# Reordering the first group of a fused FFT and GEGLU backward kernel: dO transposes, w_down products, and the life of q

## The chip, the cores and the metric

The kernel runs on one core of one Trainium2 chip. The metric is the device time of one execution in microseconds. The engines of the core are TensorE (PE, matrix products and transposes; PEld is its weight load), VectorE (DVE), ScalarE (ACT), GpSimd (POOL) and SyncE (SP, which issues transfers). They run side by side and wait for each other by semaphores.

## The reference, cut to what matters

The forward pass mixes two branches with a gate computed from `x`: a filter in the frequency domain (`a`) and a GEGLU feed-forward (`b`). Both branches and the gate read the same `x`; the input `B_x` is not used. The kernel computes the output and the gradients of the seven inputs that are used.

```python
# x: 2048 x 576, w_gate, w_up: 576 x 4608, w_down: 4608 x 576, all bf16
g = sigmoid((x * gate_w).sum(-1))
X = rfft2(x) * (w_r + 1j * w_i)
a = irfft2(X)
b = (gelu(x @ w_gate) * (x @ w_up)) @ w_down
out = g * a + (1 - g) * b
# gradients of out . grad_out for x, w_r, w_i, w_gate, w_up, w_down, gate_w
```

For the feed-forward branch the backward pass needs, with dO the incoming gradient: `z = dO @ w_down^T` (scaled by 1 - g it is `da`), the products A = gelu(xg) * xu, dH_g and dH_u, and then the weight gradients `d_w_down = A^T @ ((1-g) dO)` and `d_w_gate`, `d_w_up` = `x^T @ [dH_g, dH_u]`.

## The kernel before

The first part of the kernel goes over 18 groups of 256 hidden columns. Each group is four steps (m = 0 to 3), and a step takes 512 of the 2048 rows. So "step 9" is the first step of the third group, and the steps are counted from `pr = 0` in the code. One step makes z (16 matmuls over 128 rows of d each and 4 over the last 64), xy (gate and up products, in two halves, each in a PSUM tile of two), evacuates these with ScalarE, and works out the GELU and its derivative on VectorE. The weight gradients of a group are made in the four steps of the next group, as a list of jobs; a list of Fourier units (`fft_next`) is spread between the jobs. The z tile and the Fourier units' tile are one and the same PSUM buffer.

```python
pz = tc.tile_pool(name="pz", bufs=1, space=PSUM)    # z and the Fourier units' tile
pg = tc.tile_pool(name="pg", bufs=2, space=PSUM)    # first group: transposes and gate
pw = tc.tile_pool(name="pw", bufs=2, space=PSUM)    # later groups: weight gradients ("wps")
# ... cut ...
def H_mm(g, m, between=()):
    for t in ts:                                    # 4 x 4 matmuls of z
        for ci in range(4):
            nc.tensor.matmul(zo(t), lhsT=dOT[:, ci, t, :], rhs=wdT[:, ci, :], ...)
    for f in between:
        f()
    for t in ts:                                    # z: the last 64 rows of d; L418
        nc.tensor.matmul(zo(t), lhsT=dOT[r, 4, t, :], rhs=wdT[r, 4, :], ...)
    # ... xy: the last 64 rows of d (L422); full(k) makes the rest of half k (L429)
```

The chain on VectorE has a first part (`H_ew1`: s, q, the start of dH_g) and a second (`H_ew2`) behind the sigmoids. The tile q exists once from the second group on; ScalarE writes it from xy (`Square`, L448) in `H_act`.

```python
def H_ew2(g, m, tiles, s, dH, da):
    xb, q, hu = tiles
    one = g < 2 or m == 2
    if one:
        om = xb
        nc.scalar.activation(s[:], s[:], ACT.Sigmoid, scale=2.0 * C_GELU)
    else:
        om, s = s, ewt("sg", g)
        nc.scalar.activation(s[:], om[:], ACT.Sigmoid, scale=2.0 * C_GELU)
        nc.scalar.activation(om[:], om[:], ACT.Sigmoid, scale=-2.0 * C_GELU)
    A = keepA.tile([P, 4, FG], BF16, tag="A", name="A")
    dHg, dHu = dH[:, :, 0, :], dH[:, :, 1, :]
    V.tensor_tensor(xb[:], xb[:], s[:], op=ALU.mult)          # L483
    V.tensor_tensor(dHu, da[:], xb[:], op=ALU.mult)           # L484
    V.tensor_tensor(A[:], xb[:], hu[:], op=ALU.mult)          # L485
    V.tensor_tensor(q[:], xb[:], q[:], op=ALU.mult)           # L486
    if one:
        V.tensor_scalar(om[:], s[:], -1.0, 1.0, op0=ALU.mult, op1=ALU.add)
    V.tensor_tensor(om[:], om[:], q[:], op=ALU.mult)          # L489, last reader of q
    V.tensor_tensor(om[:], om[:], s[:], op=ALU.add)
    V.tensor_tensor(dHg, dHg, om[:], op=ALU.mult)
```

The jobs of a group are dealt to its steps by this list (entries 0 to 3: steps of the next group; entry 4: carried into the first step of the group after; entry 5: placed inside a step, before xy). `d` are the four products of d_w_down (two halves of 8 matmuls each, L535), `w` the four of d_w_gate and d_w_up (in quarters of 4 matmuls, L553).

```python
if g == 0:
    return [[w[0][:1], w[1][:1]], [w[2]], [d[0], d[1], d[2], d[3]], [w[3][:3]], w[3][3:],
            {1: [w[0][1][1], w[1][1][1]], 2: [tail]}]
```

And these are the first group's and the later groups' steps:

```python
if g == 0:
    z, xy_full = H_mm(g, m, ([opening] if m == 0 else []) + rest)
    rest = []
    da = H_da(g, m, z)
    # do2, x1: three transposing items each; dO of step m + 2, x of step m + 1
    if m == 0:
        early, mid_, late_ = do1[:2], [do1[2], x1[0]], x1[1:]
    elif m < NPR - 1:
        early, mid_, late_ = x1[:2], x1[2:], []
    for f in early: f()
    xy = xy_full(0)
    for f in mid_: f()
    # ... H_act of half 0, second half of xy, H_act of half 1 ...
    if m < NPR - 1:
        gate(m + 1)
    if m + 2 < NPR:
        do2[0]()
        do2[1]()
        rest = [do2[2]]
    state += [*H_ew1(g, tiles, da), da]
else:
    z, xy_full = H_mm(g, m)
    da = H_da(g, m, z)
    # ... inside ...
    xy = xy_full(0)
    if held:
        scale_dB(0, AC)      # (1-g) dO, rows of one quarter, on ScalarE (AC) or VectorE (VC)
        held.pop()()
    # ... H_act of half 0, xy_full(1), H_act of half 1 ...
    state += [*H_ew1(g, tiles, da), da]
    if pr == 5:
        scale_dB(1, AC)
        scale_dB(2, VC)
        build_R(nc, tb, unit, 8)
        build_R(nc, tb, unit, 12)
    elif pr == 6:
        scale_dB(3, VC)
        next(makeB)
    # ... the jobs of the step, with Fourier units between them; then H_ew2 ...
```

After the 18 groups a second part reads A and dH back from memory and makes the output and the gradient of x.

Of the kernel before, what the change touches and what calls it, by code (L numbers as in the profile page):

```python
# [10 lines left out]
ALU = mybir.AluOpType  # L11
# [244 lines left out]
def kernel(  # L256
# [7 lines left out]
    V = nc.vector  # L264
# [168 lines left out]
    def ewt(tag, g):  # L433
        if tag in ("q", "s", "sg"):
            return unit([4, FG], name=tag) if g == 0 else ew.tile([P, 4, FG], BF16, tag=tag, name=tag, bufs=1)
        return ew.tile([P, 4, FG], BF16, tag=tag, name=tag, bufs=2)
# [7 lines left out]
    def H_act(k, xy, tiles, part):  # L444
        xb, q, hu = tiles
        h = slice(2 * k, 2 * k + 2)
        if part == 0:
            nc.scalar.activation(q[:, h, :], xy[:, :, 0:FG], ACT.Square)  # L448
        else:
            nc.scalar.copy(xb[:, h, :], xy[:, :, 0:FG])  # L450
            nc.scalar.copy(hu[:, h, :], xy[:, :, FG:2 * FG])  # L451

    def H_ew1(g, tiles, da):
        xb, q, hu = tiles
        s = ewt("s", g)
        V.tensor_scalar(s[:], q[:], A_GELU, 1.0, op0=ALU.mult, op1=ALU.add)  # L456
        V.tensor_tensor(s[:], xb[:], s[:], op=ALU.mult)
        V.tensor_scalar(q[:], q[:], 6.0 * A_GELU * C_GELU, 2.0 * C_GELU, op0=ALU.mult, op1=ALU.add)
        dH = keep.tile([P, 4, 2, FG], BF16, tag="dH", name="dH")
        V.tensor_tensor(dH[:, :, 0, :], da[:], hu[:], op=ALU.mult)  # L460
        return s, dH
# [9 lines left out]
    def H_ew2(g, m, tiles, s, dH, da):  # L471
        xb, q, hu = tiles
        one = g < 2 or m == 2
        if one:
            om = xb
            nc.scalar.activation(s[:], s[:], ACT.Sigmoid, scale=2.0 * C_GELU)
        else:
            om, s = s, ewt("sg", g)
            nc.scalar.activation(s[:], om[:], ACT.Sigmoid, scale=2.0 * C_GELU)  # L479
            nc.scalar.activation(om[:], om[:], ACT.Sigmoid, scale=-2.0 * C_GELU)  # L480
        A = keepA.tile([P, 4, FG], BF16, tag="A", name="A")
        dHg, dHu = dH[:, :, 0, :], dH[:, :, 1, :]
        V.tensor_tensor(xb[:], xb[:], s[:], op=ALU.mult)  # L483
        V.tensor_tensor(dHu, da[:], xb[:], op=ALU.mult)  # L484
        V.tensor_tensor(A[:], xb[:], hu[:], op=ALU.mult)  # L485
        V.tensor_tensor(q[:], xb[:], q[:], op=ALU.mult)  # L486
        if one:
            V.tensor_scalar(om[:], s[:], -1.0, 1.0, op0=ALU.mult, op1=ALU.add)
        V.tensor_tensor(om[:], om[:], q[:], op=ALU.mult)  # L489
        V.tensor_tensor(om[:], om[:], s[:], op=ALU.add)  # L490
        V.tensor_tensor(dHg, dHg, om[:], op=ALU.mult)
        fsl = slice(g * FG, (g + 1) * FG)
        def store():
            for k, tl in ((0, A[:]), (2, dHu), (1, dHg)):
                LD.dma_start(scr[k][m][:, :, fsl].rearrange("t p f -> p t f"), tl)
        stores.append(store)
        kept.setdefault(g, []).append((A, dH))
# [16 lines left out]
    def W_units(g):  # L514
        fsl = slice(g * FG, (g + 1) * FG)
        kt = kept[g]

        def tl(k, t):
            tile_ = kt[t // 4][min(k, 1)]
            return tile_[:, t % 4, :] if k == 0 else tile_[:, t % 4, k - 1, :]  # L520
        dwd_tiles, wp = {}, {}

        def halves(f, us):
            return [(us, lambda: f(0)), (us, lambda: f(1))]

        def wtile(key):
            if key not in wp:
                wp[key] = pw.tile([P, TPB, FG], F32, tag="wps", name="wps")
            return wp[key]

        def u_dwd(fch, h):
            def f(half):
                wps = wtile(("d", fch, h)).rearrange("p a b -> p (a b)")
                for t in range(8 * half, 8 * half + 8):
                    nc.tensor.matmul(wps[:, :288], lhsT=tl(0, t)[:, fch * P:(fch + 1) * P],  # L535
                                     rhs=dB[:, t, h * 288:(h + 1) * 288], start=(t == 0), stop=(t == T - 1))
                if half == 0:
                    return
                if h == 0:
                    dwd_tiles[fch] = stage.tile([P, D], BF16, tag="dwd", name="dwd")  # L540
                dwd = dwd_tiles[fch]
                wevac(dwd[:, h * 288:(h + 1) * 288], wps[:, :288])
                if h == 1:
                    r0 = g * FG + fch * P
                    wst[0].dma_start(out_6[r0:r0 + P, :], dwd[:])
            return halves(f, 1.0)

        def u_dw(c, cuts=(0, 4, 8, 12, T)):

            def f(t0, t1):  # L550
                wps = wtile(("w", c))
                for t in range(t0, t1):
                    nc.tensor.matmul(wps[:].rearrange("p a b -> p (a b)"), lhsT=xn[:, t, c * P:(c + 1) * P],  # L553
                                     rhs=kt[t // 4][1][:, t % 4].rearrange("p k f -> p (k f)"), start=(t == 0), stop=(t == T - 1))
                if t1 < T:
                    return
                dw = dwtile("dw")
                wevac(dw[:], wps[:])
                for k, ov in enumerate((o4v, o5v)):
                    wst[0].dma_start(ov[:, c, fsl], dw[:, k, :])  # L560
            return [(3.45 * (b - a) / T, lambda a=a, b=b: f(a, b)) for a, b in zip(cuts, cuts[1:])]

        def tail():
            wps = wtile("t")
            for t in range(T):
                for k, r in ((1, LO), (2, HI)):
                    nc.tensor.matmul(wps[r, 0, :], lhsT=xn[:, t, 512:576], rhs=tl(k, t),  # L567
                                     start=(t == 0), stop=(t == T - 1))
            dw = dwtile("dwt")
            wevac(dw[:, 0], wps[:, 0, :])  # L570
            wst[0].dma_start(out_4[512:576, fsl], dw[LO, 0, :])
            wst[0].dma_start(out_5[512:576, fsl], dw[HI, 0, :])
        w = [u_dw(c, (0, 12, T)) if g == 0 and c < 2 else u_dw(c) for c in range(4)]
        d = [u_dwd(fch, h) for fch in range(FCH) for h in range(2)]
        if g == 0:
            return [[w[0][:1], w[1][:1]], [w[2]], [d[0], d[1], d[2], d[3]], [w[3][:3]], w[3][3:], {1: [w[0][1][1], w[1][1][1]], 2: [tail]}]
        return [[d[0]], [d[1], d[2], d[3]], [w[0], w[1][:2]], [w[1][2:], w[2]], w[3], {2: [tail]}]


# [306 lines left out]
    VC, AC = V.tensor_copy, nc.scalar.copy  # L886
# [5 lines left out]
    for c in range(6):  # L892
        w = gwr[0:1, eo(c)] if c < 4 else gwr[0:1, 512:D]
# [83 lines left out]
    carry, pend, held, rest = [], None, [], []  # L977

    def scale_dB(k, cp):
        for t in range(4 * k, 4 * k + 4):  # L980
            if cp == AC:
                nc.scalar.activation(dB[:, t, :], dB[:, t, :], ACT.Copy, scale=omg32[:, t:t + 1])
            else:
                V.tensor_scalar(dB[:, t, :], dB[:, t, :], omg32[:, t:t + 1], None, op0=ALU.mult)  # L984

    for g in range(NG):
# [3 lines left out]
        for m in range(NPR):  # L990
            pr = g * NPR + m
# [14 lines left out]
            if g == 0:  # L1006
# [3 lines left out]
                do2 = items(dB, dOT, m + 2, AC, AC, VC)  # L1010
                x1 = items(xn, xT, m + 1, AC if m else VC, VC, VC)
# [3 lines that stand above are left out]
                if m == 0:  # L1015
                    early, mid_, late_ = do1[:2], [do1[2], x1[0]], x1[1:]
                elif m < NPR - 1:
                    early, mid_, late_ = x1[:2], x1[2:], []
                else:
                    early, mid_, late_ = [], [], []  # L1020
                for f in early:
# [24 lines left out]
                    V.tensor_scalar(gs32[:], g32[:], SD2, None, op0=ALU.mult)  # L1046
                if m + 2 < NPR:
                    do2[0]()
                    do2[1]()
                    rest = [do2[2]]  # L1050
                state += [*H_ew1(g, tiles, da), da]
                held.append(sigs)
            else:
                z, xy_full = H_mm(g, m)
                da = H_da(g, m, z)
                for f in inside:
                    f()
                xy = xy_full(0)
                if held:
                    scale_dB(0, AC)  # L1060
# [4 lines left out]
                xy = xy_full(1, fft_next if k0 else None)  # L1065
                for part in range(2):
                    H_act(1, xy, tiles, part)
                state += [*H_ew1(g, tiles, da), da]
                if pr == 5:
                    scale_dB(1, AC)  # L1070
                    scale_dB(2, VC)
                    build_R(nc, tb, unit, 8)
                    build_R(nc, tb, unit, 12)
                elif pr == 6:
                    scale_dB(3, VC)
                    next(makeB)
                side_work(4.4)
                jobs = carry + hs
# [273 lines left out]
```

## Time and profile before

| | |
|---|---|
| Time, median of 3 runs | 1403.53 us (1403.35 to 1403.58) |
| Span of the profiled execution | 1401.2 us |
| Granted TensorE clock | 1.00 |
| Instructions | 25933 |
| First group (steps 0 to 3) | about 0 to 47 us |
| Steps 4 to 8 | about 47 to 113 us |

The busy table gives the time of each engine, its share of the span and its instructions. A list of waits gives, for each pair of waiter and releaser, the total in us, how often, and the longest. A timeline line gives start and duration in us, engine, line of the code, operation, tiles (out<-in), shape, count, and in brackets the idle time of the engine before it with what ended that. A matmul's end is modelled, as matmuls overlap each other; the starts are what was recorded, and a few records are missing.

### The profile page before, as it was taken

What the parts mean: (1) busy time and instruction counts of PE and PEld (TensorE: products, weight loads), DVE (VectorE), ACT (ScalarE), POOL (GpSimd) and SP (SyncE); (2) the same over time, 40 slices, a digit from 0 to 9 for tenths busy, and PEclk for the clock granted to TensorE, in tenths of its full rate; (3) what the DMA queues carried; (4) which work ended last, traced back from release to release, by engine and by line L of the source; (5) the groups of instructions that cost most, each with busy time, mean ns of one, the idle gap of its engine ahead of it and who ended that gap; (6) DMA issues with size and microseconds to landing.
All of it is one profiled execution on the core that took longest, in us unless ns stands there. A gap on an engine that the chain in (4) does not pass through costs nothing.

```text
span 1401.2 us, 25933 instructions
## 1 busy us (share of the span) xinstructions
PE 1373.5 (98%) x10187; PEld 913.6 (65%) x10272; DVE 748.9 (53%) x1408; ACT 710.7 (51%) x1309; POOL 245.1 (17%) x486
## 2 busy tenths in 40 slices
PE   8999999999999999999999999999999999999999
PEld 6556566565566566556566566556777777777777
DVE  7876655655888878785666666561000742212101
ACT  6867767777778778767777767661000000000000
POOL 3000111123335634422101111100000100000000
PEclk9999999999999999999999999999999999999999
DMA  7423435355455656546446465849999998878774
GB/s 216 125 80 111 126 111 135 91 145 157 109 153 142 157 155 165 129 137 164 135 135 182 119 169 136 199 110 277 193 191 191 237 190 167 161 160 167 154 152 90
DMA packets 510646, 214.49 MB, mean 153 GB/s; under 512 B 312538, under 2 KB 503708, under 8 KB 510524
## 3 DMA queue, kind: packets, MB, share of 16 engines
q1 hardware_dynamic: 493402, 187.44, 57.5%
q0 software_dynamic: 14912, 24.24, 6.3%
q8 instruction: 80, 1.31, 0.4%
q10 hardware_dynamic: 2210, 1.15, 0.3%
q14 instruction: 42, 0.34, 0.1%
HBM read 41.05 MB, written 93.84 MB: 96 GB/s over the span
## 4 chain that ended last, share of the span: by engine, by line
PE 56%; DVE 1%; ACT 1%; issue 0%; DMA 0%; SPq 0%; DVEq 0%; ACTq 0%
PE acc L1202 30%; PE wps L553 7%; PE xy L429 6%; PE wps L535 4%; PE z L413 3%; PE wps L567 1%; PE xy L422 1%; PE z L418 1%; PE pf L867 1%; PE pf L869 1%; ACT ZT L844 0%; PE pf L841 0%; ACT q L448 0%; DMA wdT<-wdT 0%; ACT Xg L710 0%
## 5 line engine op out<-in xcount | busy, mean ns | idle before, releaser
L1202 PEld LDWEIGHTS <-pin 128*128 128x128 bf16 x3456 | 338.0, 98 | 85.8 <-issue 0.5
L553 PE MATMUL wps<-dH,xn 128*128 128x512 bf16 x1137 | 269.9, 379 | 0.7
L429 PE MATMUL xy<-wgu,xT 128*128 128x512 bf16 x1082 | 258.0, 379 | 8.5 <-issue 7.1
L429 PEld LDWEIGHTS <-xT 128*128 128x128 bf16 x1152 | 106.5, 98 | 133.0 <-issue 24.8
L553 PEld LDWEIGHTS <-xn 128*128 128x128 bf16 x1152 | 111.4, 98 | 118.4 <-issue 0.6
L1219 ACT COPY bo<-acc 128x288 f32<-128x288 f32 x32 | 12.8, 399 | 305.0 <-PE acc L1202 271.6
L535 PE MATMUL wps<-dB,A 128*128 128x288 bf16 x1152 | 154.2, 286 | 1.0 <-DVE dB L984 0.9
L560 POOL DMA_DIRECT2D out_dram<-dw x134 | 72.8, 547 | 440.7 <-ACT dw L504 397.8
L1202 PE MATMUL acc<-wgT,pin 128*128 128x288 bf16 x1152 | 143.8, 286 | 0.0
L1202 PE MATMUL acc<-wuT,pin 128*128 128x288 bf16 x1152 | 143.6, 286 | 0.0
L1202 PE MATMUL acc<-wd_all,pin 128*128 128x288 bf16 x1152 | 142.6, 286 | 0.0
L413 PE MATMUL z<-wdT,dOT 128*128 128x256 bf16 x1152 | 137.5, 272 | 1.8 <-ACT ve L616 0.8
L535 PEld LDWEIGHTS <-A 128*128 128x128 bf16 x1152 | 112.1, 98 | 34.7 <-issue 1.9
L441 ACT ACTIVATE da<-z,omg 128x256 bf16<-128x256 f32 x288 | 112.3, 473 | 37.0 <-PE z L418 36.2
L413 PEld LDWEIGHTS <-dOT 128*128 128x128 bf16 x1152 | 112.5, 98 | 23.8 <-issue 3.0
L450 ACT CAST xb<-xy 128x512 bf16<-128x512 f32 x144 | 85.1, 591 | 49.0 <-PE xy L429 48.5
L1274 DVE SCALAR_TENSOR_TENSOR f32t<-gwf,dlog,b16t 128x576 f32<-128x576 f32 x16 | 13.1, 817 | 172.8 <-DMA b16t<-dxa_scr 172.8
L448 ACT ACTIVATE q<-xy 128x512 bf16<-128x512 f32 x144 | 87.7, 612 | 14.2 <-PE xy L429 4.9
L451 ACT CAST hu<-xy 128x512 bf16<-128x512 f32 x144 | 87.3, 606 | 0.0
L483 DVE TENSOR_TENSOR xb<-xb,sg 128x1024 bf16<-128x1024 bf16 x48 | 33.2, 691 | 95.5 <-ACT sg L479 95.4
L504 ACT CAST dw<-wps 128x512 bf16<-128x512 f32 x72 | 42.5, 592 | 52.5 <-PE wps L553 47.6
L456 DVE TENSOR_SCALAR s<-q 128x1024 bf16<-128x1024 bf16 x72 | 30.7, 426 | 67.1 <-ACT q L448 67.1
(216 smaller groups left out, 1635.7 us busy)
## 6 DMA issues: line engine op xcount, KB each, us to landing
scr<-dH SPq DMA_DIRECT2D x144, 256.0 KB, 3.4
scr<-A SPq DMA_DIRECT2D x72, 256.0 KB, 2.7
out_dram<-dw POOLq DMA_DIRECT2D x134, 64.0 KB, 2.6
wd_all<-in_B_w_down_dram SPq DMA_DIRECT2D x3, 1728.0 KB, 9.4
out_dram<-dwd POOLq DMA_DIRECT2D x34, 144.0 KB, 3.0
scr_p<-Vt SPq DMA_DIRECT2D x32, 145.0 KB, 2.8
wgu<-in_B_w_gate_dram SPq DMA_DIRECT2D x18, 256.0 KB, 4.0
wgu<-in_B_w_up_dram SPq DMA_DIRECT2D x18, 256.0 KB, 3.4
```

Of the source, the lines that this page charges most:

```text
L413: nc.tensor.matmul(zo(t), lhsT=dOT[:, ci, t, :], rhs=wdT[:, ci, :], start=(t % 4 < 2 and ci == 0), stop=False)
L429: nc.tensor.matmul(xy[k][:, t % 2, :], lhsT=xT[:, ci, t, :], rhs=wgu[:, ci, :], start=False, stop=(ci == 3))
L441: nc.scalar.activation(da[:, t, :], z[:, t % 2, t // 2, :], ACT.Copy, scale=omg32[:, 4 * m + t:4 * m + t + 1])
L448: nc.scalar.activation(q[:, h, :], xy[:, :, 0:FG], ACT.Square)
L450: nc.scalar.copy(xb[:, h, :], xy[:, :, 0:FG])
L451: nc.scalar.copy(hu[:, h, :], xy[:, :, FG:2 * FG])
L483: V.tensor_tensor(xb[:], xb[:], s[:], op=ALU.mult)
L504: wcopy[0](out, in_)
L535: nc.tensor.matmul(wps[:, :288], lhsT=tl(0, t)[:, fch * P:(fch + 1) * P], rhs=dB[:, t, h * 288:(h + 1) * 288], start=(t == 0), stop=(t == ...
L553: nc.tensor.matmul(wps[:].rearrange("p a b -> p (a b)"), lhsT=xn[:, t, c * P:(c + 1) * P], rhs=kt[t // 4][1][:, t % 4].rearrange("p k f -> ...
L560: wst[0].dma_start(ov[:, c, fsl], dw[:, k, :])
L1202: nc.tensor.matmul(acc[:, :288], lhsT=src[:, r, :], rhs=w_of(r)[:, h * 288:(h + 1) * 288], start=(first and r == 0), stop=(last and r == F ...
```

## The change

It has three parts. In the first group one more dO transpose moves from behind the gate's product to the middle of the next step's z, and one x transpose moves behind the first half of xy; that is meant to leave the shared PSUM buffers time to come free. The products of d_w_down of the first group move one step forward, spread over two steps; for that the scaling of dO (`scale_dB`) is moved forward and dealt anew to ScalarE and VectorE, and half of the last d_w product goes to the ninth step (`pr = 8`), between whose Fourier units it stands. From the third group on, q's two operations stand before the products that make dH_u and A, so that q comes free for ScalarE sooner; the factor `om` takes a tile of its own where it stood in xb, which is now needed longer.

```diff
@@ H_ew2
         if one:
-            om = xb
+            om = xb if g < 2 else ewt("sg", g)
@@
+        def products():
+            V.tensor_tensor(dHu, da[:], xb[:], op=ALU.mult)
+            V.tensor_tensor(A[:], xb[:], hu[:], op=ALU.mult)
         V.tensor_tensor(xb[:], xb[:], s[:], op=ALU.mult)
-        V.tensor_tensor(dHu, da[:], xb[:], op=ALU.mult)
-        V.tensor_tensor(A[:], xb[:], hu[:], op=ALU.mult)
+        if g < 2:
+            products()
         V.tensor_tensor(q[:], xb[:], q[:], op=ALU.mult)
         if one:
             V.tensor_scalar(om[:], s[:], -1.0, 1.0, op0=ALU.mult, op1=ALU.add)
         V.tensor_tensor(om[:], om[:], q[:], op=ALU.mult)
+        if g >= 2:
+            products()
         V.tensor_tensor(om[:], om[:], s[:], op=ALU.add)
@@ W_units
-            return [[w[0][:1], w[1][:1]], [w[2]], [d[0], d[1], d[2], d[3]], [w[3][:3]], w[3][3:], {...}]
+            return [[w[0][:1], w[1][:1]], [d[0], d[1]], [d[2], d[3], w[2][:2]], [w[2][2:], w[3][:2]], w[3][2:], {...}]
@@ first group
-                    early, mid_, late_ = x1[:2], x1[2:], []
+                    early, mid_, late_ = x1[:1], x1[1:], []
@@
                     do2[0]()
-                    do2[1]()
-                    rest = [do2[2]]
+                    rest = do2[1:]
@@ later groups
                     f()
+                if pr == 5:
+                    scale_dB(2, AC)
                 xy = xy_full(0)
@@
+                if pr == 5:
+                    scale_dB(3, VC)
                 state += [*H_ew1(g, tiles, da), da]
-                if pr == 5:
-                    scale_dB(1, AC)
-                    scale_dB(2, VC)
+                if pr == 4:
+                    scale_dB(1, VC)
+                elif pr == 5:
                     build_R(nc, tb, unit, 8)
                     build_R(nc, tb, unit, 12)
                 elif pr == 6:
-                    scale_dB(3, VC)
                     next(makeB)
```

More of the change, by code (lines that the diff above doesn't have):

```diff
@@ L575, in W_units @@
         if g == 0:
-            return [[w[0][:1], w[1][:1]], [w[2]], [d[0], d[1], d[2], d[3]], [w[3][:3]], w[3][3:], {1: [w[0][1][1], w[1][1][1]], 2: [tail]}]
+            return [[w[0][:1], w[1][:1]], [d[0], d[1]], [d[2], d[3], w[2][:2]], [w[2][2:], w[3][:2]], w[3][2:], {1: [w[0][1][1], w[1][1][1]], 2: [tail]}]
         return [[d[0]], [d[1], d[2], d[3]], [w[0], w[1][:2]], [w[1][2:], w[2]], w[3], {2: [tail]}]
```

## The prediction

> **What bounds the kernel now.** I read the busy table first, then TensorE's own list of waits, then the timelines of the three compute engines around each of those waits.
>
> ```profile
> PE 1373.5 (98%) x10187; PEld 913.6 (65%) x10272; DVE 748.9 (53%) x1408; ACT 710.7 (51%) x1309; POOL 245.1 (17%) x486
> ```
>
> TensorE is busy for 1373.5 of 1401.2 us. The change neither adds nor removes a matmul, so all it can bring is part of TensorE's idle time. The list of TensorE's waits (what waited, for whom, total us, times, longest) names it:
>
> ```profile
> PE pf L378 <- ACT g_bf L396: 2.4, 3, 1.0
> PE pf L705 <- ACT Xx L710: 1.2, 2, 0.8
> PE pf L705 <- ACT Xg L710: 1.1, 1, 1.1
> PE pf L596 <- ACT ve L616: 1.1, 1, 1.1
> PE wps L535 <- DVE dB L984: 0.9, 1, 0.9
> PE pf L794 <- ACT Vt L797: 0.8, 2, 0.6
> PE z L413 <- ACT ve L616: 0.8, 1, 0.8
> PE pf L378 <- DVE dOT L385: 0.7, 1, 0.7
> PE pf L613 <- ACT Y L601: 0.6, 1, 0.6
> ```
>
> The list also has 7.1 us of "issue" before L429 in 45 pieces of at most 0.2 us. In the timeline these stand where a group of 16 shows 15 matmuls, so they are mostly missing records, and I count nothing for them. On the other side a listed wait is too short: matmul starts are 213 ns apart for 512 columns while each is shown as 379 ns long, so about 0.166 us of each true stop hides under a modelled end. I therefore add 0.166 us to each wait. The timeline of the first and second steps shows what the transposes wait for:
>
> ```profile
> 30.41 0.61 PE L378 MATMUL pf<-ident,dB 128*128 128x128 bf16 x8
> 31.80 0.61 PE L378 MATMUL pf<-ident,dB 128*128 128x128 bf16 x8 [0.78 <-ACT g_bf L396]
> 36.43 0.61 PE L378 MATMUL pf<-ident,xn 128*128 128x128 bf16 x8 [0.75 <-DVE dOT L385]
> ```
>
> And the timeline near 393 us, far from the first group, shows a second mechanism:
>
> ```profile
> 392.62 0.69 DVE L489 TENSOR_TENSOR s<-s,q 128x1024 bf16<-128x1024 bf16 x1
> 393.35 0.60 ACT L448 ACTIVATE q<-xy 128x512 bf16<-128x512 f32 x1 [0.99 <-DVE s L489]
> 393.84 1.27 ACT L710 CAST Xx<-pf 64x578 bf16<-64x578 f32 x2
> 397.03 1.28 ACT L710 CAST Xx<-pf 64x578 bf16<-64x578 f32 x2
> 398.37 0.41 PE L705 MATMUL pf<-Vp,Btab 128*128 128x289 bf16 x2 [0.83 <-ACT Xx L710]
> ```
>
> ScalarE cannot write the new q until VectorE has read the old one at L489. From 393.35 to 398.31 ScalarE then runs without a pause, and TensorE waits at its end for the Fourier evacuation.
>
> **What the Trainium skill says.** "TensorE: Matmul & The Clock Gate", section "Single matmul latency", gives a fixed part of 166 ns of one matmul, and "Back-to-back issue gap" an N/2.4 spacing; the trace agrees: 379 less 213 is 166. "Perfetto Trace Analysis", section "Tensor Engine Instruction (MATMUL, LD_WEIGHTS)", calls ACT and DVE strict FIFO; the block above agrees, since one held q delays the unrelated evacuations behind it. "VectorE: DVE Perf Modes", section "The DRAIN you can't avoid", says a semaphore between Vector operations costs nothing extra; this trace differs: at 128x1024 the next start comes after 0.61 us where nothing is waited for (29.44 to 30.05) and after 0.72 us where the operand was just made (28.72 to 29.44).
>
> **Part 1, the transposes of dO.** Steps 0 and 1 of the first group end with the gate's product and two dO transposes. These share two PSUM buffers: the second transpose takes the gate's buffer, which ScalarE frees only after its evacuations of xy. The change puts it behind the 16 z products of the next step (16 x 0.107 = 1.71 us), and one of two x transposes behind the first xy half. The stops concerned are 0.68, 0.78 and 0.75 us, each plus 0.166: 2.71 us. New waits, worked out by laying the same durations (evacuation 1.03 us, starts 0.90 apart) behind each other: the third dO transpose takes the first one's buffer and meets its evacuation, about 0.1 to 0.25 us; the x transpose of step 1 about 0.2; that of step 2 about 0.4, because its buffer is evacuated by VectorE, which is busy without a pause from 28.72 to 36.4. That leaves 1.8 us by the gate of step 3 (40.55 becomes 38.75).
>
> VectorE then caps it. From 39.37 to 67.78 us it idles under 0.8 us. Its chain starts when the last x copy is done, at 38.0 for 39.37, so 1.37 us sooner. Through s (L457) and the sigmoid it sets ScalarE's evacuation of step 3 and so the wait at 49.80 (0.24 us), which grows to about 0.7. Part 1: -1.4 us at step 4.
>
> **Part 2, the w_down products and the scaling of dB.** In the kernel before, this is the stop on the last quarter of dB:
>
> ```profile
> 80.85 1.20 DVE L984 TENSOR_SCALAR dB<-dB,omg 128x576 bf16<-128x576 bf16 x4
> 81.27 7.18 PE L535 MATMUL wps<-dB,A 128*128 128x288 bf16 x52 [0.94 <-DVE dB L984]
> 95.98 0.67 ACT L601 CAST Y<-pf 128x580 bf16<-128x580 f32 x1
> 96.71 0.41 PE L613 MATMUL pf<-Y,Rt 128*128 128x290 bf16 x2 [0.59 <-ACT Y L601]
> 100.77 1.91 PE L413 MATMUL z<-wdT,dOT 128*128 128x256 bf16 x16 [0.79 <-ACT ve L616]
> 109.94 0.91 PE L596 MATMUL pf<-Dt,xT 128*128 128x290 bf16 x6 [1.06 <-ACT ve L616]
> ```
>
> The four tiles of the quarter cost 0.94 + 0.166 and then about 0.16 three times: 1.6 us. The change starts these products one step sooner, at 66.56 - 1.4 = 65.2 us, with tile 12 of dB due at 65.2 + 12 x 0.12 = 66.6. The scaling of dB by VectorE now stands behind the end of step 4's chain: 67.78 - 1.4 + 1.2 (another quarter, now ahead of that chain) - 0.2 (a pause it fills) = 67.4, so its tiles are ready from 67.7 to 68.6. The products end at 68.8 rather than 67.1: the stop moves, 1.6 us before and about 1.7 after. I count -1.6 + 1.7.
>
> One new stop in step 6: the half of a d_w product that now stands there takes the PSUM buffer of the third w_down product, whose evacuation on VectorE follows the table work of 2 us. That work would run from 81.6 to 83.5, the copy to 84.0, while TensorE is through at 83.3: +0.75 us.
>
> Steps 7 and 8: four pieces of d_w for three in step 7, so the last piece (4 x 0.213 = 0.85 us) stands behind the last Fourier product, and the stop of 0.79 + 0.166 falls to about 0.1: -0.85. The stop of 0.59 stays, as the first Fourier unit still has one piece behind it while ScalarE is evacuating. In step 8 there are two pieces for one, one of them now ahead of the first Fourier product: the stop of 1.06 + 0.166 falls to about 0.4: -0.8. Part 2 in sum: +0.1 + 0.75 - 0.85 - 0.8 = -0.8 us.
>
> **Part 3, q freed early.** From the third group on, the products of q come right behind the first product of the chain, and the two that make dH_u and A after them. q is then free two operations sooner, 2 x 0.61 = 1.2 us and some. ScalarE's waits for q on VectorE stand in the timeline before six of TensorE's late stops; a stop shrinks by the smaller of the wait, 1.3 us, and itself:
>
> - 382.39: stop 0.60 + 0.17, wait 1.84: -0.77
> - 398.37: 0.83 + 0.17, wait 0.99: -0.97
> - 449.55: 0.24 + 0.17, wait 0.99: -0.41
> - 477.02: 1.11 + 0.17, wait 0.58: -0.58
> - near 578: 0.41 + 0.17, wait 0.54: -0.54
> - near 591: 0.41 + 0.17, wait 0.26: -0.26
>
> That is -3.5 us. A and dH_u come 1.3 us later, but are first used about four us after that at the earliest, and mostly steps later. The third step of a group needs a buffer of its own for the factor, which is free by then.
>
> **The sum.** -1.4 - 0.8 - 3.5 = -5.7 us; 1403.53 - 5.7 = 1397.8.
>
> **The rivals.** First, the first group is bound by VectorE and ScalarE, so parts 1 and 2 return nothing: VectorE is at 8.67 of 10.9 us from 28.5 to 39.4 and 17.16 of 18.0 from 60 to 78. What speaks against it is that VectorE itself waits for the transposes (1.26 us at 39.03), so an earlier transpose starts its chain earlier. Then only part 3 remains: about 1400. Second, the dB scaling hurts more than it did: on ScalarE another quarter (2.8 us) now precedes step 5's evacuations, on VectorE a quarter precedes step 4's chain, and if xy of step 6 waits for them too, the first group loses one or two us: about 1401. Third, the freed stops are all returned, those of 0.59 and at 81.6 to 84.0 included, because TensorE starts later and lets ScalarE catch up: -9 us, about 1394.5. Fourth, part 3 only moves ScalarE's wait: had q no work behind it, nothing would be gained; the unbroken run from 393.35 to 398.31 speaks against it.
>
> **Range and chances.** Part 3 rests on waits seen directly; I give it 2.5 to 4. The first group rests on sums of chained durations with errors near 1 us at each of four places; I give it +0.5 to -4.5. Together 1395.3 to 1400.8 holds it 8 times in 10. Two per cent would be 28 us, over all of TensorE's idle time, and nothing suggests a loss of that size.
>
> **What would show it.** The waits of L378 for g_bf fall from three to the one at the start; the wait of L535 for dB appears near 68 instead of 81; a wait of L553 for a dwd copy near 83; the z wait of 0.79 vanishes, that of 1.06 halves; ScalarE's waits for L489 nearly vanish, and L705 and L794 wait under 1 us together. It would be wrong if TensorE waits for xy evacuations between 60 and 80 us by more than 1 us, or if new waits come up after 200 us.

## The result and the profile after

The changed kernel takes 1395.57 us (1395.51 to 1396.09), the kernel before in the same session 1403.44 us: the ratio is 0.9944, with a 95% interval of 0.9931 to 0.9957. That is 7.9 us less, with an interval of about 6.0 to 9.7; the forecast was 5.7 less, and its range (1395.3 to 1400.8) holds the time near its lower end.

The busy table of the changed kernel (time of each engine, share of the span of 1394.3 us, instructions recorded):

```profile
PE 1372.9 (98%) x10186; PEld 914.3 (66%) x10272; DVE 740.2 (53%) x1406; ACT 710.8 (51%) x1311; POOL 245.6 (18%) x486
```

TensorE's work is what it was; the span shrank by idle time alone. TensorE's waits in the changed kernel (waiter, releaser, total us, times, longest; the lines have moved by up to eight, so L378 is the same and L535 is now L541):

```profile
PE pf L378 <- ACT g_bf L396: 1.0, 1, 1.0
PE pf L619 <- ACT Y L607: 0.7, 1, 0.7
...
PE xy L422 <- ACT hu L451: 0.6, 1, 0.6
PE wps L541 <- DVE dB L990: 0.6, 1, 0.6
PE pf L711 <- ACT Xg L716: 0.5, 1, 0.5
...
PE wps L559 <- DVE dwd L510: 0.5, 1, 0.5
...
PE pf L602 <- ACT ve L622: 0.2, 1, 0.2
...
PE pf L378 <- DVE dOT L385: 0.2, 1, 0.2
```

Of the waits for the gate one is left, the one in step 0 that the change does not touch. The waits on Xx and Vt are gone, of the two on Xg one is gone and the larger has halved, that on ve in step 8 is 0.22 for 1.06, and the z wait on ve is gone. New is the wait for dwd, and the wait for hu has grown from 0.24 to 0.61. In TensorE's timeline of the kernel before it was this line:

```profile
49.80 0.39 PE L422 MATMUL xy<-wgu,xT 64*128 64x512 bf16 x2 [0.24 <-ACT hu L451]
```

After 200 us no new wait has come up, and between 60 and 80 us TensorE waits for no evacuation of xy: neither of the prediction's two signs of being wrong is there.

The list says which waits went, but not how many us each place returned, since modelled ends and missing records blur it. A sharper reading is to take from each timeline the start of each step's first z product, which is recorded in full (1152 of 1152 matmuls), and to subtract. This table holds the changed kernel or an experiment minus the kernel before, one profiled execution of each, in us, with the difference at step 0's start taken out (the executions differ there by up to 0.54 us):

| start of step | 1 | 2 | 4 | 5 | 6 | 7 | 9 | 29 | 30 | 35 | 37 | 46 |
|---|---|---|---|---|---|---|---|---|---|---|---|---|
| changed kernel | -1.28 | -2.05 | -2.01 | -1.64 | +0.07 | -3.25 | -3.16 | -4.09 | -5.18 | -5.86 | -6.53 | -7.42 |
| part 1 alone | -1.28 | -2.05 | -2.02 | -1.65 | -1.65 | -1.65 | -1.65 | -1.65 | -1.65 | -1.67 | -1.67 | -1.76 |
| part 2 alone | 0 | 0 | 0 | 0 | +1.69 | -1.62 | -1.52 | -1.52 | -1.53 | -1.47 | -1.46 | -1.46 |
| part 3 alone | 0 | 0 | 0 | 0 | 0 | 0 | 0 | -0.94 | -2.04 | -2.72 | -3.39 | -4.29 |
| q released late | -1.29 | -2.06 | -2.03 | -1.66 | +0.05 | -3.27 | -3.18 | -3.48 | -3.68 | -4.00 | -4.12 | -4.52 |

Read along a row: a number that stays is a stretch in which nothing changed. (Of the +1.69 at step 6, about 0.45 is work moved forward, 32 short products in step 5 for 16 of another kind, and 1.24 is the stop on dB that moves with it; step 6 is shorter by 3.3 in return.) The three parts add up to -7.5 us by step 46, the whole change to -7.42, and both lie in the interval of the times.

TensorE's timeline in the first group of the changed kernel:

```profile
30.29 0.61 PE L378 MATMUL pf<-ident,dB 128*128 128x128 bf16 x8
30.73 1.91 PE L413 MATMUL z<-wdT,dOT 128*128 128x256 bf16 x16
32.48 0.61 PE L378 MATMUL pf<-ident,dB 128*128 128x128 bf16 x8
36.68 0.61 PE L378 MATMUL pf<-ident,xn 128*128 128x128 bf16 x8 [0.17 <-DVE dOT L385]
48.70 0.39 PE L422 MATMUL xy<-wgu,xT 64*128 64x512 bf16 x2 [0.61 <-ACT hu L451]
```

The second dO transpose now follows 1.75 us of z products and waits for nothing; the x transpose waits 0.17 for 0.75. The last line is where VectorE's pace takes 0.4 us of it back. And in steps 5 to 8:

```profile
67.70 3.08 PE L541 MATMUL wps<-dB,A 128*128 128x288 bf16 x20 [0.61 <-DVE dB L990]
83.85 1.89 PE L559 MATMUL wps<-dH,xn 128*128 128x512 bf16 x7 [0.47 <-DVE dwd L510]
94.09 0.41 PE L619 MATMUL pf<-Y,Rt 128*128 128x290 bf16 x2 [0.68 <-ACT Y L607]
97.20 1.02 PE L559 MATMUL wps<-dH,xn 128*128 128x512 bf16 x4
98.15 1.91 PE L413 MATMUL z<-wdT,dOT 128*128 128x256 bf16 x16
107.32 0.91 PE L602 MATMUL pf<-Dt,xT 128*128 128x290 bf16 x6 [0.22 <-ACT ve L622]
```

The stop on dB has moved from 81 to 68 us, the new one on dwd is at 84, and the stop before the z of step 8 is filled by the four d_w matmuls at 97.20.

Where q is freed early, all engines' timeline of the changed kernel at the place shown before:

```profile
386.93 0.69 DVE L490 TENSOR_TENSOR q<-xb,q 128x1024 bf16<-128x1024 bf16 x1
387.72 0.69 DVE L493 TENSOR_TENSOR s<-s,q 128x1024 bf16<-128x1024 bf16 x1
...
388.70 0.62 ACT L448 ACTIVATE q<-xy 128x512 bf16<-128x512 f32 x1
...
389.19 1.29 ACT L716 CAST Xx<-pf 64x578 bf16<-64x578 f32 x2
...
392.39 1.28 ACT L716 CAST Xx<-pf 64x578 bf16<-64x578 f32 x2
...
393.73 0.41 PE L711 MATMUL pf<-Vp,Btab 128*128 128x289 bf16 x2
```

The last reader of q (L493) ends at 388.41, before ScalarE gets to q at 388.70, and neither ScalarE's Square nor TensorE's L711 carries a bracket. ScalarE's waits for q between 300 and 900 us in the kernel before were these, and the changed kernel has none of them:

```profile
ACT q L448 <- DVE s L489: 4.1, 4, 1.8
...
ACT q L448 <- DVE xb L489: 2.8, 5, 0.9
```

### The profile page after: what moved, and what is told of

Read it like the earlier page. It is cut to its first block, busy times and chain, and to the rows that moved or that the text cites. A ratio compares the mean times of both kernels' runs of the same rounds, so it can differ in the third digit from the quotient of the medians.

```text
span 1394.3 us, 25930 instructions
## 1 busy us (share of the span) xinstructions
PE 1372.9 (98%) x10186; PEld 914.3 (66%) x10272; DVE 740.2 (53%) x1406; ACT 710.8 (51%) x1311; POOL 245.6 (18%) x486
## 3 DMA queue, kind: packets, MB, share of 16 engines
q8 instruction: 80, 1.31, 0.4%
## 4 chain that ended last, share of the span: by engine, by line
PE 90%; ACT 2%; issue 1%; DMA 0%; SPq 0%; DVE 0%; ACTq 0%
PE acc L1210 30%; PE wps L559 16%; PE xy L429 15%; PE wps L541 9%; PE z L413 8%; PE wps L573 2%; PE xy L422 2%; PE pf L602 2%; PE z L418 1%; PE pf L619 1%; PE pf L873 1%; PE pf L800 1%; PE pf L711 1%; PE pf L875 1%; ACT ZT L850 0%
## 5 line engine op out<-in xcount | busy, mean ns | idle before, releaser
L429 PE MATMUL xy<-wgu,xT 128*128 128x512 bf16 x1083 | 258.2, 379 | 8.3 <-issue 7.0
L429 PEld LDWEIGHTS <-xT 128*128 128x128 bf16 x1152 | 106.5, 98 | 133.0 <-issue 24.8
L541 PE MATMUL wps<-dB,A 128*128 128x288 bf16 x1152 | 154.2, 286 | 0.7 <-DVE dB L990 0.6
L541 PEld LDWEIGHTS <-A 128*128 128x128 bf16 x1152 | 112.1, 98 | 34.3 <-issue 1.3
```

Source lines behind the costliest of these rows:

```text
L429: nc.tensor.matmul(xy[k][:, t % 2, :], lhsT=xT[:, ci, t, :], rhs=wgu[:, ci, :], start=False, stop=(ci == 3))
```

## The experiments

The theory is the one of the prediction: TensorE's idle pieces are separate stops, each with its own cause, and they add. Its rivals are that VectorE bounds the first group as a whole, that the late gain is a matter of phase, and that the order of VectorE's chain counts and not the release of q. The moves inside part 1 and inside part 2 were not run apart from each other; what each is worth is read from the steps.

**Part 1 alone.** The kernel before with the two edits of the first group only.

```diff
-                    early, mid_, late_ = x1[:2], x1[2:], []
+                    early, mid_, late_ = x1[:1], x1[1:], []
-                    do2[1]()
-                    rest = [do2[2]]
+                    rest = do2[1:]
```

> The kernel before with part 1 alone (one dO transpose moved into the next step's z, one x transpose behind the first half of xy). Adding stops: the steps up to the fourth gain what they gained in the changed kernel, 2.0 us by step 3, of which the grown wait for hu in step 4 takes 0.4, so -1.6 us; VectorE's chain is sooner by about the same, so the stop on the last quarter of dB near 80 us stays at 1.6 us and takes nothing more: 1401.8. Rival, everything up to step 6 is bound by VectorE and the gain is only to be had with part 2: within 0.4 us of before, with a longer stop on dB near 80.

Measured 1401.73 us, ratio 0.9989 (0.9982 to 0.9996): -1.8 us. TensorE's timeline of this run:

```profile
48.16 0.39 PE L422 MATMUL xy<-wgu,xT 64*128 64x512 bf16 x2 [0.61 <-ACT hu L451]
```
```profile
79.63 2.59 PE L535 MATMUL wps<-dB,A 128*128 128x288 bf16 x16 [0.95 <-DVE dB L984]
```

The stop on dB is 0.95 where it was 0.94: TensorE and VectorE came forward together, so nothing was given back there. The cap in step 4 is real, but it takes 0.37 of 2.02 us. The rival falls.

**Part 2 alone.** The kernel before with the new list of jobs and the scaling of dB only.

```diff
-  [..., [w[2]], [d[0], d[1], d[2], d[3]], [w[3][:3]], w[3][3:], ...]
+  [..., [d[0], d[1]], [d[2], d[3], w[2][:2]], [w[2][2:], w[3][:2]], w[3][2:], ...]
   # scale_dB: 1 on VectorE in step 4, 2 on ScalarE and 3 on VectorE in step 5
```

> The kernel before with part 2 alone (w_down products one step sooner, dB scaled sooner, half of a d_w product to the ninth step). Adding stops: the stop on dB moves to step 5 and is 1.3 to 1.7 us, a new one of 0.6 on an evacuation by VectorE in step 6, the z wait of step 7 (0.95 us) goes and that of step 8 shrinks by 0.8: -1.5 us, 1402.0. Rival, without part 1 VectorE is later by 1.4 us at the dB scaling and the stop in step 5 grows to 3 us: about 1403.5, no gain.

Measured 1401.81 us, ratio 0.9987 (0.9978 to 0.9995): -1.75 us. Its timeline in step 5:

```profile
69.11 3.08 PE L535 MATMUL wps<-dB,A 128*128 128x288 bf16 x20 [0.60 <-DVE dB L984]
```

0.60 without part 1 and 0.61 with it: again the two engines move together, and the stop is not the 3 us of the rival.

**Part 3 alone.** The kernel before with the new `H_ew2` only.

> The kernel before with part 3 alone (q freed early from the third group on). Adding stops: ScalarE's waits for q vanish and six steps between 380 and 600 us are shorter by 0.94, 1.09, 0.69, 0.67, 0.52 and 0.37 us, as in the changed kernel: -4.3 us, 1399.2, and the first 380 us as before. Rival, the late gain is one of phase and comes from the first group's reordering: within 0.5 us of before.

Measured 1399.38 us, ratio 0.9971 (0.9959 to 0.9982): -4.2 us. In the step table nothing moves up to step 9 and then -0.94, -1.10, and so on to -4.29, with the same numbers as in the changed kernel. The late gain needs nothing from the first group.

**q released late.** The changed kernel with the two products put back between q's operations.

```diff
         V.tensor_tensor(q[:], xb[:], q[:], op=ALU.mult)
+        if g >= 2:
+            products()
         ...
         V.tensor_tensor(om[:], om[:], q[:], op=ALU.mult)
-        if g >= 2:
-            products()
```

> The changed kernel with the two products of part 3 put between q's own two operations: the first operation on q is early as in the changed kernel, but the last reader of q ends as late as in the kernel before. If the release of q is what counts: ScalarE's waits on VectorE for q come back with 0.5 to 1.8 us and the gain of part 3 is lost, +4 us to about 1399.6. Rival, the chain on VectorE is better packed (each product stands where its operand is not the one just made): the gain stays, 1395.6 within 0.5.

Measured 1399.35 us, ratio 0.9970 (0.9958 to 0.9981). Its timeline at the same place:

```profile
390.01 0.60 ACT L448 ACTIVATE q<-xy 128x512 bf16<-128x512 f32 x1 [0.79 <-DVE s L495]
...
393.70 1.28 ACT L716 CAST Xx<-pf 64x578 bf16<-64x578 f32 x2
...
395.04 0.41 PE L711 MATMUL pf<-Vp,Btab 128*128 128x289 bf16 x2 [0.78 <-ACT Xx L716]
```

The chain of wait, unbroken evacuations and stop is back, with ScalarE's wait at 0.79 where it was 0.99 in the kernel before and zero in the changed one. From step 9 to step 46 this kernel gains 1.34 of part 3's 4.26 us. So the release accounts for about two thirds (2.9 us), and the rest is a piece of the rival: even with the release as late by position, q's last reader ends up to 0.3 us sooner (the longest wait of ScalarE is 1.5 us for 1.8). It no longer stands directly behind the operation that makes its operand: near 390 us it starts 0.60 us after the operation ahead of it, where in the kernel before it was 0.79 (391.83 to 392.62).

**The last quarter of dB ahead of step 4's chain.**

```diff
                 if pr == 4:
                     scale_dB(1, VC)
+                    scale_dB(3, VC)
-                if pr == 5:
-                    scale_dB(3, VC)
```

> The changed kernel with the last quarter of dB scaled on VectorE ahead of step 4's chain instead of behind it. If the stop in step 5 is only VectorE's queue order: the tiles are ready at about 63 us, the stop of L541 on dB (0.61 shown, 1.25 us with what hides and the three small ones) vanishes and nothing takes its place: -1.2 us against the changed kernel, 1394.3. Rival, step 4's chain, 1.2 us later, holds q and xb for ScalarE's evacuations of step 5 and these hold z and xy of step 6: no gain, 1395.6.

Measured 1394.37 us, ratio 0.9936 (0.9920 to 0.9953). The step table moves by -1.24 us against the changed kernel, in step 5 alone. All engines' timeline of this run:

```profile
60.59 2.32 DVE L990 TENSOR_SCALAR dB<-dB,omg 128x576 bf16<-128x576 bf16 x8
...
65.05 4.08 PE L541 MATMUL wps<-dB,A 128*128 128x288 bf16 x32
```

All 32 products run without a bracket. The stop was the place of four operations in VectorE's queue, not VectorE's load.

**The gate's stop in step 0.** The second dO transpose behind four matmuls of xy.

```diff
-                    early, mid_, late_ = do1[:2], [do1[2], x1[0]], x1[1:]
+                    early, mid_, late_ = do1[:1], [do1[2], x1[0]], x1[1:]
-                xy = xy_full(0)
+                xy = xy_full(0, do1[1] if m == 0 else None)
```

> The changed kernel with part 1's means used once more: in step 0 the second dO transpose stands after four matmuls of xy instead of directly behind the first, so that the gate's PSUM buffer has 0.86 us to come free. Stop of 0.97 + 0.17 us at 15 us shrinks by 0.86: 1394.7. Rival, VectorE's chain sets the pace from step 0 on and the wait for hu in step 4 grows by the same: 1395.6.

Measured 1396.06 us, ratio 0.9947 (0.9932 to 0.9962): no gain. From step 1 to the last the step table is that of the changed kernel to 0.04 us; behind it this execution waits 0.6 us for a transfer, which that of the changed kernel does not. The wait for the gate has left the list (by starts it is 0.27 us for 1.13), and two others stand within 2.5 us of it, 0.48 and 0.38 us by starts, which is all of the 0.86. TensorE's waits from 12 to 20 us, and VectorE's timeline there:

```profile
PE pf L394 <- ACT xT L385: 0.4, 1, 0.4
PE pf L384 <- DVE dOT L385: 0.3, 1, 0.3
PE pf L378 <- DVE dOT L385: 0.2, 1, 0.2
```
```profile
14.49 1.14 DVE L165 SCALAR_TENSOR_TENSOR XR<-kk,scol 128x128 int32<-128x128 f32 x4
15.66 0.43 DVE L172 TENSOR_SCALAR XR<-XR 128x512 int32<-128x512 int32 x1
16.01 1.61 DVE L385 COPY dOT<-pf 128x1024 bf16<-128x1024 bf16 x3
```

The wait of L394 is also in the changed kernel. VectorE makes tables until 16 us and only then empties the transposes. The rival was right that VectorE takes the gain, but not by the place it named: the wait for hu in step 4 is 0.61 as before. The same means that worked in steps 1 and 2 fails where the next thing in line is just as late.

**Table work first.** In step 6, 2 us of table work on VectorE ahead of the first part of the chain (`next(makeB)` moved up in front of `H_ew1`).

> The changed kernel with the 2 us of table work on VectorE in step 6 put ahead of the first part of the chain, into a pause in which VectorE waits for q. The copy of the third w_down product then comes as soon as that product is done, and the stop of L559 on that copy (0.47 + 0.17 us) vanishes: 1395.0. Rival, the chain of step 6, 0.6 to 2 us later, delays the sigmoid and the stops come back there: 1395.6 or more.

Measured 1395.55 us, ratio 0.9947 (0.9932 to 0.9962): no gain. In the step table step 6 is 0.63 us shorter, as expected, and step 7 is 0.58 longer. TensorE's timeline of step 7 in this run, and ScalarE's:

```profile
93.61 0.41 PE L619 MATMUL pf<-Y,Rt 128*128 128x290 bf16 x2 [1.31 <-ACT Y L607]
```
```profile
90.96 1.09 ACT L448 ACTIVATE q<-xy 128x512 bf16<-128x512 f32 x2 [0.88 <-DVE xb L493]
```

The stop on Y grew from 0.68 to 1.31. ScalarE waits for q: the mechanism of part 3, in the second group, which part 3 leaves out.

**The Fourier unit between the halves of xy in step 7.** One number: `pr > 7` becomes `pr > 6`.

> The changed kernel with step 7's first Fourier unit between the two halves of xy, as in all later steps. Its evacuation then stands ahead of the second half's on ScalarE: the stop of L619 on Y (0.68 + 0.17 us) vanishes, and one like that of step 8 (0.22 + 0.17) comes: -0.45 us, 1395.1. Rival, ScalarE is the bound of that stretch and the order does not matter: 1395.6.

Measured 1395.22 us, ratio 0.9944 (0.9929 to 0.9958). Against the changed kernel, step 7 is 0.53 us shorter, and from step 1 on nothing else differs; in the times that is inside the scatter. Step 0 is 1.7 us longer in the profiled execution, the slowest of the four: the clock granted to TensorE from 14 to 19 us is 0.66 in it and 1.00 in that of the changed kernel, so this is no effect of the move.

**Table work first, and q freed early from the second group on.** The run with the table work first, and the three bounds of part 3 set from 2 to 1.

> The run with the table work first, with part 3 extended to the second group (step 7 is in it). In that run the stop on the copy went and the stop of L619 on Y grew from 0.68 to 1.31 us, as ScalarE waited 0.88 us for q on VectorE. If that wait is why: freeing q 1.3 us sooner takes it away, the Y stop shrinks to about 0.4 and the whole is 0.9 us under the changed kernel: 1394.7. Rival, ScalarE is held by its table loads and sines in step 6 and would be as late without the wait for q: 1395.5.

Measured 1394.94 us, ratio 0.9943 (0.9929 to 0.9957). ScalarE's and TensorE's timelines at the same place:

```profile
90.86 0.60 ACT L448 ACTIVATE q<-xy 128x512 bf16<-128x512 f32 x1 [0.15 <-PE xy L429]
```
```profile
93.02 0.41 PE L619 MATMUL pf<-Y,Rt 128*128 128x290 bf16 x2 [0.59 <-ACT Y L607]
```

ScalarE now waits for TensorE and not for q, the stop is 0.59 for 1.31, and steps 5, 6 and 7 are shorter than in the changed kernel by 0.25, 0.63 and 0.14 us, 1.0 in sum. So the wait for q was the cause. The forecast of 0.4 for the stop was too good.

**Two moves, and all moves.** The changed kernel with dB ahead of the chain and the unit between the halves; then that with the table work first and q freed early from the second group on.

> The changed kernel with the last quarter of dB ahead of step 4's chain and step 7's first Fourier unit between the halves of xy. Adding stops: -1.24 and -0.5 us against the changed kernel: 1393.8. Rival, step 7 is set by ScalarE once TensorE is sooner by 1.2 us: 1394.3.

> The two moves together with the table work first and part 3 from the second group on. Adding stops: -1.24 for dB, -0.63 for the copy, -0.5 for Y: -2.4 us against the changed kernel, 1393.2. Rival, the stops of steps 6 and 7 are one delay of ScalarE and not two: 1393.8 as with two moves.

Measured 1393.95 us, ratio 0.9936 (0.9923 to 0.9948), with steps of -1.24 and -0.53; and 1393.16 us (1393.12 to 1393.44), ratio 0.9930 (0.9918 to 0.9943), with -1.24, -0.61 and -0.58 us in steps 5 to 7, where the expectation had -1.24, -0.63 and -0.5. The all-moves kernel is the fastest of this study, 9.9 us under the kernel before in its session where the changed kernel was 7.9 under; the intervals of the two ratios overlap, and it is the steps that show the difference. Its busy table, from an execution of which all 10272 matmuls were recorded, follows. Its list of waits has no "issue" before L429, where the kernel before had 7.1 us: those were missing records, as the prediction had it.

```profile
PE 1380.2 (99%) x10272; PEld 913.1 (66%) x10272; DVE 739.5 (53%) x1406; ACT 710.1 (51%) x1311; POOL 245.2 (18%) x486
```

## Why the prediction came out as it did

- *Only TensorE's idle time can be won, and the stops add.* Right: the three parts alone give -1.8, -1.75 and -4.2 us, -7.8 in sum, and the change -7.9.
- *Part 1: 1.8 us by step 3, capped by VectorE to 1.4.* Right in kind and nearly in size: 2.0 and 1.65. The wait for hu was to grow to about 0.7 and is 0.61, and the x transpose of step 2 waits 0.17 instead of 0.4.
- *Part 2: -0.8.* Right in kind at each of its places, too small in sum: it is -1.5 by the steps. The term furthest off is the moved stop on dB, put at 1.7 us by a chain of VectorE durations. It is 0.61 shown, about 1.25 with what hides, because VectorE reached the tiles about 0.6 us sooner than the chain had it. The old stop on dB, counted as 1.6, was 1.75 by starts, and the stop on dwd was put at 0.75 and is 0.63 by starts.
- *Part 3: -3.5.* Right in kind, too small in size: -4.3, outside the 2.5 to 4 that the prediction gave it. The sum went through the waits list, which holds no stop that the modelled end hides nearly whole. In the kernel before, the last of the 16 matmuls at 444.69 ends at 446.81 by the model and L794 starts at 446.93; that gap of 0.12 is in no list, and it was a stop of 0.28 us counted by starts. Step 33 returned 0.69 us where one listed stop of 0.41 had been counted. The better packed chain, shown by the run with q released late, is the other part: step 44 returned 0.37 for 0.26, more than ScalarE's whole wait. TensorE's timeline of the kernel before at the first of these places:

```profile
444.69 2.12 PE L535 MATMUL wps<-dB,A 128*128 128x288 bf16 x16
446.93 0.41 PE L794 MATMUL pf<-qm,BTtab 128*128 128x290 bf16 x2
```

- *What hides under a modelled end: 0.166 us.* Close. The trace has the starts of 512-column matmuls 216 ns apart, and not 213 as the prediction reads them, so 163 ns hide; no term changes by more than 0.01 us.
- *The rivals.* VectorE as the bound of the first group, the dB scaling that costs more than it brings, and a late gain that is only moved: none holds. "All stops returned" (-9) is also too much: those on Y, dwd and dB stayed.
- *The range.* All three sizes were too small, so the errors added: the measured time is 0.3 us above the lower end of the range. The mechanism was right; that the range held is owed to the width given to the first group (+0.5 to -4.5, measured -3.2), which made up for part 3.

## What to carry to other kernels

When one engine is full at 98%, list its stops one by one and ask of each whose queue order it is: four operations moved ahead in another engine's queue were worth 1.2 us here, with no work removed. A buffer that exists once is freed by its last reader, so put that reader first, above all where an in-order engine has unrelated work behind the wait. And compare kernels by the starts of a repeated instruction: per step that resolves 0.05 us where the times scatter by half a microsecond and more. The six late steps that part 3 shortens have the same length to 0.01 us in the nine kernels here that hold part 3 as it is or more of it, and so do not hang on one execution. The start and the end of an execution do differ, by up to 1.7 and 1.0 us, and belong left out.

## What the runs showed that was not expected

The order of dependent and independent operations on VectorE shows outside VectorE. What is left of part 3 with q's last reader at its old position, the packing and the factor's own tile, was worth 1.34 us between steps 9 and 46, although VectorE is busy only 53% of the time; 1.03 of it stands in four steps where q's last reader belongs to a step with no change of tile, so that packing alone is left. And 0.86 us taken from one wait in step 0 came back whole at two others behind it, since two queues there were late by almost the same.
